# Score masks of the first batch written into PSUM by TensorE, maximum and difference by VectorE from there, the last stores over two queues, and a new order of the instructions

## The chip, the cores and the metric

The kernel runs on one core of one Trainium2 chip. The metric is device time in microseconds (us), lower is better. The engines are TensorE (PE, with its weight loads PEld), VectorE (DVE), ScalarE (ACT), GpSimd (POOL) and SyncE (SP), which issues nearly all DMAs.

## The reference

A sparse attention over 8 heads is followed by a mixture of 4 attention experts. Batch 8, 576 tokens, 8 heads of 64.

```
# stage 1: heads 0-3 see the last 32 tokens, heads 4-7 every 32nd token
scores = 0.125 * q @ k.T
mask_local = (rel >= 0) & (rel < 32)
mask_strided = (rel >= 0) & (pos_k % 32 == pos_q % 32)
scores = where(mask, scores, -1e9); scores -= max(scores)
attn = exp(scores) / (sum(exp(scores)) + 1e-9)
x = concat_heads(attn @ v)                                   # (8, 576, 512)
# stage 2: 4 experts, the best two of a token weighted by a softmax of x @ w_gate
for e in range(4):
    q, k, v = x @ wq[e], x @ wk[e], x @ wv[e]
    a = causal softmax of 0.125 * q @ k.T
    out += gate weight of e * (a @ v @ wo[e])
```

## The kernel before, in words

Stage 1 works on pairs of heads: pairs 0 and 1 of a batch are local, pairs 2 and 3 strided. For a pair q and k are loaded, and in batches 0 and 1 TensorE transposes them (`tp`, L611, L624, L640) and ScalarE or VectorE copies the result from PSUM to `qkt` (`tp_out`, through the helper `copy`, L345). TensorE computes the scores in small blocks, as many as are needed (L673 local, L689 strided), into two PSUM banks `sp`, one for each head. The softmax follows: VectorE adds the mask and writes to SBUF (`p`, L703), takes the maximum (L714), GpSimd subtracts it (L716), ScalarE takes the exponential (L718), VectorE the sums (L720) and their inverse (L723, L725), and GpSimd multiplies (L727). In batch 0 all but the inverse is done head by head. The result is transposed (by VectorE for local pairs, L743, into `pt`; by TensorE for strided ones, L753, and copied), multiplied with v (L783, L802) into `xa`, and split into a high and a low part `xh` and `xl` (L765 ScalarE, L767 VectorE).

Stage 2 projects `xh` and `xl` with the split weights (`wh_k`, `wl_k` and so on, split at L455 and L457). For the first pair of experts of batch 0 the projections are separate matmuls for each head pair (L977), elsewhere in one piece (L966, L895). Then come the experts' scores (L1047, L1059, L1081), masks and maxima (L1016), exponentials (L1021), transposes (L1144), values (L1183) and the output projection (`yp`, L1217), whose result is copied to `ys` and stored (L1227 to L1233).

Nothing of this runs in the order in which it is written. Each step is recorded by `op` (kind, the engines that can do it, what it reads and writes), and `schedule` issues the steps in the order of the table `ORDER`. `SECOND` names the steps that go to their second engine, and `FILL` says before which steps TensorE is given dummy matmuls of 512 columns (L305), whose result nobody reads. Every engine works through its queue in that order, so an instruction that waits holds all behind it. Each queue thus follows the tables; a table's change moves instructions on all engines.

The constants are made first on GpSimd and VectorE: `ident`, `m_loc` (mask of local scores), `m_str` (of strided), and, as steps, `m_cau`, `m_sw` and `m_last` for stage 2.

Of the kernel before, what the change touches and what calls it, by code (L numbers as in the profile page):

```python
# [22 lines left out]
def attention_moe_kernel(  # L23
# [60 lines left out]
    class Ring:  # L84
# [36 lines left out]
    }  # L121
    ORDER = [
# [136 lines left out]
    ]  # L259
    FILL = {  # L260
        7: 1, 17: 7, 80: 4, 132: 3, 134: 3, 139: 1, 216: 2,
    }

    def op(kind, eng, key, fn, r=(), w=(), mode=None, dmas=(), after=()):
# [73 lines left out]
    def dve(n):  # L338
        return 0.07 + 0.00104 * n
# [42 lines left out]
    for hf in range(2):  # L382
        v_ = m_str[64 * hf:64 * hf + 64].rearrange("p (g u) -> p g u", u=NJ)
        keep(v_, [[-NJ, 3], [-1, NJ]], 0, 1)
        keep(v_, [[NJ, 3], [0, NJ]], NJ - 1, -1)
# [909 lines left out]
```

## Time and profile before

The median of three runs is 422.71 us (422.70 to 422.73).

| | |
|---|---|
| the profiled execution's own time | 422.69 us |
| its span (first to last instruction) | 421.0 us |
| TensorE busy | 411.0 us, 98% |
| VectorE busy | 339.8 us, 81% |
| ScalarE busy | 277.5 us, 66% |
| GpSimd busy | 230.3 us, 55% |
| TensorE's granted clock | 0.999 of full |
| chain that ended last: PE, DVE, ACT, DMA | 86%, 5%, 3%, 2% |

The page cuts the span in 40 slices and gives the busy tenths of each engine. TensorE has an 8 in the first three slices (0 to 31.6 us) and a 6 in the last; all between are 9, which stands for 90% and more. The dummy matmuls are counted as busy. The rows below say which stretch, engine or line they are of; a bracket at the end of a row is the idle time before it and what ended it.

### The profile page before, as it was taken

What the parts mean: (1) busy time and instruction counts of PE and PEld (TensorE: products, weight loads), DVE (VectorE), ACT (ScalarE), POOL (GpSimd) and SP (SyncE); (2) the same over time, 40 slices, a digit from 0 to 9 for tenths busy, and PEclk for the clock granted to TensorE, in tenths of its full rate; (3) what the DMA queues carried; (4) which work ended last, traced back from release to release, by engine and by line L of the source; (5) the groups of instructions that cost most, each with busy time, mean ns of one, the idle gap of its engine ahead of it and who ended that gap; (6) DMA issues with size and microseconds to landing.
All of it is one profiled execution on the core that took longest, in us unless ns stands there. A gap on an engine that the chain in (4) does not pass through costs nothing.

```text
span 421.0 us, 18647 instructions
## 1 busy us (share of the span) xinstructions
PE 411.0 (98%) x7523; PEld 358.8 (85%) x7523; DVE 339.8 (81%) x1073; ACT 277.5 (66%) x877; POOL 230.3 (55%) x398
## 2 busy tenths in 40 slices
PE   8889999999999999999999999999999999999996
PEld 5668988987898879998899888998899888997775
DVE  4897898999998899978976699898988896339840
ACT  5677378668776457877767465765666469657862
POOL 5674673776536750699229630589216671185540
PEclk9999999999999999999999999999999999999999
DMA  6667637554656655464356524750443040001033
GB/s 178 194 192 181 121 91 136 100 89 96 112 102 109 146 126 87 94 129 103 72 90 133 134 46 114 129 107 11 114 102 97 20 116 22 2 26 27 27 101 100
DMA packets 156502, 41.86 MB, mean 99 GB/s; under 512 B 146080, under 2 KB 149792, under 8 KB 156416
## 3 DMA queue, kind: packets, MB, share of 16 engines
q1 hardware_dynamic: 156272, 40.54, 43.9%
q8 instruction: 59, 0.97, 1.0%
q14 instruction: 27, 0.22, 0.2%
q10 hardware_dynamic: 144, 0.13, 0.1%
HBM read 31.20 MB, written 9.44 MB: 97 GB/s over the span
## 4 chain that ended last, share of the span: by engine, by line
PE 86%; DVE 5%; ACT 3%; DMA 2%; issue 1%; POOL 1%; SPq 0%; ACTq 0%; POOLq 0%
PE bank L966 22%; PE bank L1217 12%; PE bank L1183 10%; PE bank L895 10%; PE bank L1144 6%; PE bank L1059 5%; PE bank L783 3%; PE bank L802 3%; PE bank L1047 2%; PE bank L689 2%; PE bank L673 2%; PE bank L1081 2%; PE bank L753 2%; PE bank L977 1%; DMA p<-in_q_dram 1%
## 5 line engine op out<-in xcount | busy, mean ns | idle before, releaser
L1021 ACT ACTIVATE p<-p,st 128x384 f32<-128x384 f32 (+3 forms) x128 | 71.5, 561 | 10.8 <-DVE st L1016 10.7
L1117 POOL TENSOR_SCALAR p<-p,st,wt 128x256 f32<-128x256 f32 (+2 forms) x96 | 63.9, 672 | 15.1 <-DVE st L1108 7.4
L1016 DVE CUSTOM_DVE_ANT_0 p<-bank,m_cau 128x384 f32<-128x384 f32 (+2 forms) x96 | 50.0, 548 | 1.2 <-PE bank L1059 0.6
L1183 PE MATMUL bank<-th,vs 128*64 128x192 f32 (+4 forms) x512 | 48.0, 337 | 0.0
L563 DVE STREAM_TRANSPOSE qkt<-nat 128x576 f32<-128x576 f32 x48 | 47.5, 1002 | 0.1
L1183 PEld LDWEIGHTS bank<-th,vs 128*64 128x64 f32 x512 | 33.8, 137 | 13.8 <-issue 7.1
L345 ACT COPY th<-bank 128x256 f32<-128x256 f32 (+2 forms) x108 | 40.4, 434 | 7.6 <-PE bank L1144 7.2
L765 ACT CAST xh<-bank 128x128 fp32r<-128x128 f32 (+4 forms) x112 | 29.4, 320 | 22.3 <-PE bank L783 12.8
L966 PE MATMUL bank<-xh,wh_k 128*128 128x256 f32 (+1 forms) x120 | 36.3, 303 | 0.0
L895 PE MATMUL bank<-wh_v,xh 128*128 128x260 f32 x128 | 36.2, 283 | 0.0
L895 PE MATMUL bank<-wl_v,xh 128*128 128x260 f32 x128 | 36.2, 283 | 0.0
L966 PE MATMUL bank<-xh,wh_q 128*128 128x256 f32 (+1 forms) x120 | 36.1, 301 | 0.1
L767 DVE TENSOR_TENSOR xl<-bank,xh 128x128 fp32r<-128x128 f32 (+4 forms) x112 | 31.8, 322 | 5.3 <-ACT xh L765 5.0
L895 PE MATMUL bank<-wh_v,xl 128*128 128x260 f32 x128 | 35.9, 281 | 0.0
L966 PE MATMUL bank<-xl,wh_k 128*128 128x256 f32 (+1 forms) x120 | 35.5, 296 | 0.0
L966 PE MATMUL bank<-xh,wl_k 128*128 128x256 f32 (+1 forms) x120 | 35.5, 296 | 0.0
L966 PE MATMUL bank<-xl,wh_q 128*128 128x256 f32 (+1 forms) x120 | 35.5, 296 | 0.0
L966 PE MATMUL bank<-xh,wl_q 128*128 128x256 f32 (+1 forms) x120 | 35.5, 296 | 0.0
L1144 PEld LDWEIGHTS bank<-ident,p 64*128 64x128 f32 x800 | 30.2, 139 | 5.7 <-issue 1.3
L716 POOL TENSOR_TENSOR p1l<-p1l,st 128x640 f32<-128x640 f32 (+1 forms) x18 | 20.7, 1151 | 25.7 <-DVE st L714 25.5
L1144 PE MATMUL bank<-ident,p 64*128 64x64 f32 x800 | 33.7, 226 | 0.5 <-DVE p1l L703 0.3
L727 POOL TENSOR_TENSOR p1l<-p1l,st 128x640 f32<-128x640 f32 (+1 forms) x18 | 20.5, 1141 | 18.6 <-DVE st L725 15.2
(190 smaller groups left out, 1220.1 us busy)
## 6 DMA issues: line engine op xcount, KB each, us to landing
nat<-in_q_dram SPq DMA_DIRECT2D x96, 72.0 KB
nat<-in_k_dram SPq DMA_DIRECT2D x96, 72.0 KB
out_dram<-ys SPq DMA_DIRECT2D x23, 256.0 KB
v<-in_v_dram SPq DMA_DIRECT2D x96, 40.0 KB
out_dram<-ys SPq DMA_DIRECT2D x25, 128.0 KB
v<-in_v_dram SPq DMA_DIRECT2D x48, 54.0 KB
v<-in_v_dram SPq DMA_DIRECT2D x32, 48.0 KB
v<-in_v_dram SPq DMA_DIRECT2D x32, 45.0 KB
```

The lines of the kernel that those rows point to most:

```text
L345: (nc.scalar.copy if e == "ACT" else nc.vector.tensor_copy)(dst, src)
L563: op("tq", {"DVE": 0.66 if local else 1.11}, k0 - 13, lambda e, x=x: nc.vector.transpose(turned(qkt.t, x), raw(x) if local else raw(x).rea ...
L765: op("xh", {"ACT": act(n_) + 0.04 * (not local)}, key, lambda e, s_=s_, x_=x_: nc.scalar.copy(x_(xh.t), s_(xa.t)), r=[xa], w=[xh[u]])
L767: op("xl", {"DVE": dve(n_)}, key + 0.5, lambda e, s_=s_, x_=x_: nc.vector.tensor_sub(x_(xl.t), s_(xa.t), x_(f(xh.t))), r=[xa, xh[u]], w=[x ...
L895: nc.tensor.matmul(vp.t[:, :NV], xx.t[:, t0:t0 + 128], ww.t[:, kt, :], start=i == 0, stop=i == 11)
L966: nc.tensor.matmul(pj.t[:, :n_], ww.t[:, kt, ep * 128:(ep + 1) * 128], xx.t[:, c], start=i == 0, stop=i == 11)
L1016: op("max2", {"DVE": 0.08 + 0.00104 * nk}, k_ + 0.5, lambda e, a=a: nc.vector.tensor_tensor_reduce(out=p.t[:, a, :nk], in0=sp[a].t[:, so:s ...
L1021: op("exp2", {"ACT": 0.285 + 0.00084 * nk}, k_ + 1, lambda e, a=a: nc.scalar.activation(p.t[:, a, :nk], p.t[:, a, :nk], AF.Exp, bias=st.t[ ...
L1117: lambda e, p=p, a=a, ci=ci, t=t, nk=nk, s_=s_, ep=ep: nc.gpsimd.tensor_scalar(p.t[:, a, :nk], p.t[:, a, :nk], s_.t[:, 20 + ci + a:21 + ci ...
L1144: nc.tensor.transpose(tp[hf].t[:, 64 * c:64 * c + 64], src, ident[r, r])
L1183: nc.tensor.matmul(acc.t[o, c0:c0 + cn], vw, th[ep, a].t[:, s0:s0 + cn], start=j == 0, stop=j == nj - 1, skip_group_check=True)
L1217: nc.tensor.matmul(yp.t[:, :n_], xx.t[:, c0:c0 + 128], ww.t[:, ep, c], start=i == 0, stop=i == 5)
```

## The change

In batch 0 a step `mk` is added for each head pair: for each of the pair's two banks one bf16 matmul of an identity with the mask (320 columns for a local pair, 324 for a strided one), which starts the accumulation. The score matmuls of batch 0 then accumulate onto it. The addition of the mask on VectorE (L703) goes for batch 0. The maximum is taken from PSUM, and the difference is made by VectorE from PSUM with its result in SBUF; GpSimd no longer subtracts there. Three copies to bf16 (`identb`, `m_strb`, `m_locb`) are made by ScalarE at the start. Stores of the last batch that consist of two transfers become two steps, each of which can go to SP or ScalarE. Batches 1 to 7 keep the mask on VectorE and the difference on GpSimd. `ORDER`, `SECOND` and `FILL` are replaced.

```diff
-        3, 48, 49, 50, 55, 57, 59, 60, 56, 62, 58, 52, 54, 185, 5, 7, 61, 53, 9, 51, 8, 64, 6, 17, 19, 63, 12, 13,
...
     FILL = {
-        7: 1, 17: 7, 80: 4, 132: 3, 134: 3, 139: 1, 216: 2,
+        23: 4, 36: 8, 95: 2, 101: 3, 240: 1,
     }
...
+    m_locb = const.tile([128, 5, 64], BF16, name="m_locb")
+    m_strb = const.tile([128, 54], BF16, name="m_strb")
+    identb = const.tile([128, 128], BF16, name="identb")
+    for x, y in ((identb, ident), (m_strb, m_str), (m_locb, m_loc)):
+        nc.scalar.copy(x, y)
...
+        if b == 0:
+
+            def masked(e):
+                for x in range(2):
+                    nc.tensor.matmul(sp[x].t[:, :ni * nk], identb, m_locb.rearrange("p i c -> p (i c)") if local else
+                                     m_strb.unsqueeze(1).to_broadcast([128, 6, 54]), start=True, stop=False, skip_group_check=True)
+
+            op("mk", {"PE": 0.3}, k0 - 12, masked, w=[*sp], mode=M128)
+
+        kept = {"start": b > 0, "stop": True, "skip_group_check": b == 0}
...
-                            nc.tensor.matmul(o, lhs, rhs, start=True, stop=True)
+                            nc.tensor.matmul(o, lhs, rhs, **kept)
...
-        for h in range(2):
+        for h in range(2 if b else 0):
             op("mask", {"DVE": dve(N // 2)}, k0 - 10, lambda e, h=h: nc.vector.tensor_tensor(
...
-            if step == 0:
+            if b == 0 and step < 2:
+                S_ = sp[h_[0]].t[:, :ni * nk].rearrange("p (i c) -> p i c", c=nk)
+                if step:
+                    nc.vector.tensor_tensor(pv()[:, h_[0]], S_, sv(0)[:, h_[0]].unsqueeze(2).to_broadcast([128, ni, nk]), ALU.subtract)
+                else:
+                    nc.vector.tensor_reduce(sv(0)[:, h_[0]], S_, axis=mybir.AxisListType.X, op=ALU.max)
+            elif step == 0:
...
+            def store(e, parts, c=c):
+                for dst, r in parts:
+                    (nc.scalar if e == "ACT" else nc.sync).dma_start(dst, ys.t[r, c])
+
+            for y, ps in enumerate([[x] for x in parts] if end else [parts]):
+                op("store", {"SP": 0.5, "ACT": 0.5} if end else {"SP": 0.5}, key + h + 1 + 0.1 * y, lambda e, ps=ps, store=store: store(e, ps),
+                   r=[ys[h]], dmas=[(0.4, 0.8 / len(parts))] * len(ps))
```

The tables move instructions in the whole program; three places matter below. The number at a row's start is its place in the engine's queue; the number at a name's end tells tiles apart.

The first is VectorE's queue behind the constants. Before, it copies parts of both local pairs (`qkt_170`, `qkt_172`) and then adds the mask to the first pair's scores:

```order
20 L345 COPY qkt_170<-bank_64 64x64x4 x2
21 L345 COPY qkt_172<-bank_67 64x64x4
22 L345 COPY qkt_172<-bank_68 64x128
23 L345 COPY qkt_172<-bank_69 64x64x4 x2
24 L703 TENSOR_TENSOR p1l_72<-bank_70,m_loc 128x320
25 L714 TENSOR_REDUCE st_184<-p1l_72 128x5
```

In the changed kernel the same queue begins like this (`qkt_176` is the first pair's, `qkt_178` the second's):

```order
20 L344 COPY qkt_176<-bank_64 64x64x4 x2
21 L344 COPY qkt_176<-bank_65 64x64x4
22 L344 COPY qkt_176<-bank_64 64x64x4
23 L344 COPY qkt_176<-bank_65 64x64x4 x2
24 L344 COPY qkt_178<-bank_71 64x64x4
25 L734 TENSOR_REDUCE st_190<-bank_68 128x5
26 L732 TENSOR_TENSOR p1l_72<-bank_68,st_190 128x320
27 L344 COPY qkt_178<-bank_64 64x64x4 x3
```

VectorE now makes six copies of the first pair instead of two, and maximum (L734) and difference (L732) of the first head stand among the copies of the second pair.

The second place is VectorE's transpose of the second local pair (`pt_183` before, `pt_189` after), and what stands ahead of it. Before:

```order
43 L720 TENSOR_REDUCE st_188<-p1s_176 128x6 x2
44 L723 TENSOR_REDUCE st_188<-st_188 128x12
45 L725 RECIPROCAL st_188<-st_188 128x12
46 L767 TENSOR_TENSOR xl_197<-bank_65,xh_192 128x128
47 L767 TENSOR_TENSOR xl_197<-bank_66,xh_192 128x160
48 L743 STREAM_TRANSPOSE pt_183<-p1l_73 128x640
49 L703 TENSOR_TENSOR p1s_179<-bank_71,m_str 128x6x54
50 L714 TENSOR_REDUCE st_190<-p1s_179 128x6
51 L703 TENSOR_TENSOR p1s_179<-bank_68,m_str 128x6x54
```

In the changed kernel (`p1s_185` and `st_196` are the last strided pair's):

```order
46 L734 TENSOR_REDUCE st_196<-bank_71 128x6
47 L745 TENSOR_REDUCE st_192<-st_192 128x10
48 L747 RECIPROCAL st_192<-st_192 128x10
49 L734 TENSOR_REDUCE st_196<-bank_66 128x6
50 L792 TENSOR_TENSOR xl_203<-bank_68,xh_198 128x160
51 L742 TENSOR_REDUCE st_194<-p1s_182 128x6 x2
52 L732 TENSOR_TENSOR p1s_185<-bank_71,st_196 128x6x54
53 L745 TENSOR_REDUCE st_194<-st_194 128x12
54 L747 RECIPROCAL st_194<-st_194 128x12
55 L732 TENSOR_TENSOR p1s_185<-bank_66,st_196 128x6x54
56 L792 TENSOR_TENSOR xl_203<-bank_64,xh_198 128x128
57 L768 STREAM_TRANSPOSE pt_189<-p1l_73 128x640
```

The last strided pair's two maxima and two differences have moved ahead of the transpose.

The third place is the end of ScalarE's queue. Before, ScalarE issues one store:

```order
714 L345 COPY ys_150<-bank_65 128x512
715 L345 COPY ys_151<-bank_68 128x512
716 L345 COPY ys_149<-bank_71 128x256
717 L345 COPY ys_149<-bank_67 128x256
718 L1233 DMA out_dram<-ys_149 128x256
```

In the changed kernel it issues two, and one of the two 256-column copies has gone to VectorE:

```order
706 L344 COPY ys_155<-bank_71 128x512
707 L344 COPY ys_157<-bank_67 128x512
708 L1259 DMA out_dram<-ys_157 64x512
709 L344 COPY ys_156<-bank_70 128x256
710 L1259 DMA out_dram<-ys_156 128x256
```

The store at row 708 stood in SP's queue before.

## Rows read from the trace of the kernel before

**Rows 1.** Busy time by stretch: length, PE, PEld, DVE, ACT, POOL, clock, DMA
```profile
0.00:30.00 30.00, 25.70 (x583) 18.00 (x586) 22.35 (x78) 20.06 (x55) 18.71 (x55) 1.00 0.67 185
8.42:36.91 28.49, 25.47 (x753) 19.59 (x751) 25.52 (x68) 20.21 (x59) 16.11 (x37) 1.00 0.69 195
120.00:400.00 280.00, 279.15 (x4901) 248.17 (x4901) 229.77 (x733) 185.27 (x602) 152.52 (x250) 1.00 0.39 85
400.00:417.00 17.00, 16.95 (x180) 13.06 (x178) 5.72 (x17) 9.22 (x27) 5.10 (x7) 1.00 0.29 91
417.00:421.00 4.00, 0.00 (x0) 0.00 (x0) 0.00 (x0) 0.37 (x1) 0.00 (x0) 0.89 0.54 140
```

**Rows 2.** The chain that ended last: start, length, what
```profile
7.57 1.51 PE bank L305 x7
...
20.82 1.12 POOL p1l L727 x2
...
22.18 1.42 POOL p1s L727 x2
...
24.99 0.69 POOL p1s L716
25.68 1.27 issue
...
26.98 0.74 POOL p1s L716
```

**Rows 3.** VectorE in order of time: start, length, line, output from input
```profile
6.01 0.54 DVE L378 COPY m_loc<-m_loc 128x64 f32<-128x64 f32 x4 [3.24 <-POOL m_loc L362]
...
8.42 2.68 DVE L345 COPY qkt<-bank 64x256 f32<-64x256 f32 x6 [1.81 <-ACT qkt L345]
...
22.25 0.84 DVE L743 STREAM_TRANSPOSE pt<-p1l 128x640 f32<-128x640 f32 x1
...
36.09 0.82 DVE L457 TENSOR_TENSOR wl_q<-th,wh_q 128x256 fp32r<-128x256 f32 x1
```

**Rows 4.** GpSimd in order of time, the constants
```profile
2.31 0.57 POOL L391 MEMSET m_cau<- 128x576 f32 x1
...
4.62 0.29 POOL L362 TENSOR_SCALAR_AFFINE_SELECT m_cau<-m_cau 128x128 f32<-128x128 f32 x1
...
6.92 0.23 POOL L362 TENSOR_SCALAR_AFFINE_SELECT m_loc<-m_loc 32x64 f32<-32x64 f32 x1
```

**Rows 5.** ScalarE in order of time, its first copies
```profile
5.89 4.73 ACT L345 COPY qkt<-bank 64x256 f32<-64x256 f32 x11 [3.82 <-PE bank L611]
```

**Rows 6.** Three lines up to 45 us: shortest/median/longest ns, first and last start
```profile
L703 DVE TENSOR_TENSOR p1l<-bank,m_loc x8: 474/480/492, 11.1 to 37.2; 128x320 f32<-128x320 f32 x8
L714 DVE TENSOR_REDUCE st<-p1s x4: 448/484/491, 17.4 to 26.4; 128x6 f32<-128x324 f32 x4
L716 POOL TENSOR_TENSOR p1s<-p1s,st x4: 730/732/736, 18.1 to 27.0; 128x324 f32<-128x324 f32 x4
```

**Rows 7.** TensorE in order of time
```profile
6.79 0.78 PE L611 MATMUL bank<-ident,p 128*128 128x128 f32 x4
...
22.96 0.40 PE L753 MATMUL bank<-ident,p1s 64*128 64x64 f32 x6 [0.52 <-POOL p1s L727]
...
24.66 1.17 PE L783 MATMUL bank<-pt,v 32*64 32x32 f32 x84
...
42.12 0.77 PE L1047 MATMUL bank<-qk 64*64 64x64 f32 x16
```

**Rows 8.** The last stores: copies on ScalarE, issues on SP and ScalarE
```profile
416.24 0.47 SPq L1227 DMA_DIRECT2D out_dram<-ys  x1
...
416.99 0.37 ACT L345 COPY ys<-bank 128x256 f32<-128x256 f32 x1 [0.29 <-PE bank L1217]
417.40 0.40 ACTq L1233 DMA_DIRECT2D out_dram<-ys  x1
417.44 0.54 SPq L1233 DMA_DIRECT2D out_dram<-ys  x1
```

More of the change, by code (lines that the diff above doesn't have):

```diff
@@ L688, in scores @@
                             lhs, rhs = qg(0, hf ^ x, g, 54), qg(1, hf ^ x, g, 54)
-                        nc.tensor.matmul(o, lhs, rhs, start=True, stop=True)
-        op("sl" if local else "s", {"PE": 0.72 if local else 0.66}, k0 - 11, scores, r=[qkt[0], qkt[1], *([nat[0], nat[1]] if quad and not local else [])], w=[*sp, p[0], p[1]], mode=MS if local else MQ)
+                        nc.tensor.matmul(o, lhs, rhs, **kept)
+        op("sl" if local else "s", {"PE": 0.72 if local else 0.66}, k0 - 11, scores, r=[qkt[0], qkt[1], *([nat[0], nat[1]] if quad and not local else []), *(sp if b == 0 else [])], w=[*sp, p[0], p[1]], mode=MS if local else MQ)
         N = 2 * ni * nk
@@ L738, in stage1 @@
                 r_, w_ = ((ph, sh), (ph + sh, ph), (ph, ph), (ph, sh), (sh, sh), (ph + sh, ph))[step]
+                if b == 0 and step < 2:
+                    eng = {"DVE": dve(n_)}
+                    r_, w_ = [[sp[h_[0]]], [sp[h_[0]], *sh]][step], [sh, ph][step]
                 op(f"softmax{step}", eng, k0 - 9 + step, lambda e, step=step, h_=h_: softmax(step, h_, e), r=r_, w=w_)
@@ L1221, in out_tile @@
             op("yp_out", either(n_), key + h + 0.5, lambda e, yp=yp, c=c: copy(e, ys.t[:, c], yp.t[:, :n_]), r=[yp], w=[ys[h]])
-            def store(e, c=c):
-                t0 = QT[t][0]
-                dma = nc.scalar if e == "ACT" else nc.sync
-                if last:
-                    dma.dma_start(out[b - 1, t0:, :], ys.t[:64, :])
-                    dma.dma_start(out[b, t0:, :], ys.t[64:, :])
-                elif t == 0:
-                    dma.dma_start(out[b, 64:128, :], ys.t[:64, :])
-                    dma.dma_start(out[b, :64, :], ys.t[64:, :])
-                else:
-                    dma.dma_start(out[b, t0:t0 + 128, c], ys.t[:, c])
-            op("store", {"SP": 0.5, "ACT": 0.5} if b == B - 1 else {"SP": 0.5}, key + h + 1, store, r=[ys[h]], dmas=[(0.4, 0.4)] * 2 if last or t == 0 else [(0.4, 0.8)])
+            t0 = QT[t][0]
+            end = b == B - 1
+            if last:
+                parts = [(out[b - 1, t0:, :], slice(0, 64)), (out[b, t0:, :], slice(64, 128))]
+            elif t == 0:
+                parts = [(out[b, 64:128, :], slice(0, 64)), (out[b, :64, :], slice(64, 128))]
+            else:
+                parts = [(out[b, t0:t0 + 128, c], slice(0, 128))]
+            def store(e, parts, c=c):
[4 more added lines that the diff above has]
+                   r=[ys[h]], dmas=[(0.4, 0.8 / len(parts))] * len(ps))
     for hp in START:
```

294 rows, old and new, of tables (ORDER, SECOND) are left out of this document.

## The prediction

> **What bounds the kernel now.** I read the busy time by stretch first. TensorE is busy 279.15 of 280 us from 120 to 400 and 16.95 of 17 up to 417 [rows 1]: there it alone sets the time, and as its matmuls stay the same, a new order can give back little. It is not full in two places. In the first 30 us it is busy 25.70, so 4.30 us are idle, and part of the busy time is filling: 21 dummy matmuls, which in a row of seven take 1.51 us, so 0.216 each [rows 2] and 4.5 in all. Up to the first expert scores at 42.12 [rows 7] some 8.8 us are thus not work. At the end TensorE does nothing for the last 4.0 us [rows 1].
>
> What holds TensorE up at the start is read from the chain of waits. From 20.8 to 27.7 it runs over GpSimd: normalisations (L727), then the last strided pair's two differences (L716), 0.69 and 0.74 us with 1.27 between them [rows 2]. But the stretch from 8.42 to 36.91 shows a second limit beside it: VectorE is busy 25.52 of 28.49 us, GpSimd only 16.11 [rows 1]. The chain names GpSimd; the fuller engine is VectorE. So taking GpSimd off the chain is worth only what VectorE can use.
>
> **The change part by part.** The sum is made against the profiled execution, 422.69 us, of which 1.69 lie around the span of 421.0; the median, 422.71, is the same within 0.02.
>
> *Softmax of batch 0.* VectorE loses 8 mask additions and gains 8 differences. A mask addition, which reads PSUM and a second operand, takes 0.480 us, a maximum from SBUF 0.484 to 0.488 [rows 6]. The difference reads the same operands as the addition, so I cost it at 0.48: VectorE's work is unchanged, 0 us. A maximum from PSUM is not in the trace; the nearest rows are the addition, which reads PSUM (0.48), and the maximum from SBUF (0.484). I take no change; the bounds are those two rows' extremes for one instruction, 0.448 and 0.492 [rows 6], so 8 x 0.044 = 0.35 us either way.
>
> [...]
>
> GpSimd loses 8 differences of 0.73, 5.9 us [rows 6]. On the chain stand only the last two, with the wait between: 25.0 to 27.7, 2.7 us [rows 2]. VectorE is next in line there.
>
> *Masks on TensorE.* Eight matmuls of 320 or 324 columns: at the dummies' 0.216 for 512 columns, 0.135 each, 1.1 us. Three dummies fewer give back 0.65. Both lie in the 8.8 us that are not work; if that cover is gone, the price is 1.1 us.
>
> *Constants.* ScalarE now copies three constants ahead of its first copy of transposes, which began at 5.89 [rows 5]. The last needs the finished local mask, ready at 7.15 before (6.92 + 0.23) [rows 4]; the clearing and cutting of `m_cau` that stood ahead on GpSimd, 0.57 and 0.29, has moved back, so it is ready at about 6.3, and with a 0.4 copy (a copy's length, 4.73/11) ScalarE starts at 6.7, 0.8 late. VectorE covers it: in its new queue six copies of the first pair stand at the head, where before it waited 1.81 us for ScalarE and began at 8.42 [rows 3]. It can now begin at about 5.85, when TensorE's first transposes are there (ScalarE's first copy waited for them until 5.89 [rows 5]); the mask copies of 6.01 to 6.55 [rows 3] come 0.86 earlier and are done by then. The second pair's q, which TensorE took at 6.79 [rows 7], is now loaded behind the first v; this is covered, since the first scores must wait for six copies, until about 8.5.
>
> *VectorE's account up to the last split of the first projections (36.09 + 0.82 = 36.91).* It starts 2.57 us earlier (8.42 - 5.85). It makes four more copies of transposes up to there (17 for 13), 2.68/6 = 0.45 each: 1.8. Were its 2.97 us of idle time unchanged (28.49 - 25.52), it would finish 0.8 earlier. The idle time can shrink: waits on exponentials that queue behind GpSimd are part of it. It can also grow: the first maximum now stands behind a copy and must await the first scores, and the first sum an exponential that queues behind copies on ScalarE. I take 0.7 earlier; ends: 1.75 earlier, if the GpSimd stretch of 2.7 shrinks to two VectorE differences (2.7 - 2 x 0.48), and 1.5 later (third rival). From there to the first expert scores TensorE has about as many projections and transposes left as before and is nearly full, so what VectorE gives goes through: **-0.7 us**.
>
> *The body.* The number of runs of one kind of matmul on TensorE falls from 304 to 297; from 120 to 400 only 0.85 us are idle [rows 1]. A new order can win at most about that and can lose as much by new waits: 0, between -0.7 and +0.7.
>
> *The last stores.* TensorE ends at 417.0; the copy takes 0.37, and ScalarE issues the store at 417.40. SP, held by two stores issued from 416.24, issues its last only at 417.44, for 0.54 us, up to 417.98 [rows 8]. With one of those two on ScalarE, SP is done about 0.5 earlier. ScalarE can take it: it idled 0.29 before its last copy, and another copy of that size, 0.37, goes to VectorE, which leaves 0.66 for an issue of 0.47 [rows 8]. Then ScalarE's store, issued by 417.80, is last, 0.18 earlier, with less queued ahead of it. **-0.3 us**, between 0 and -0.5.
>
> [...] I claim no more than issue time; if the data were the limit the term would be 0 and the time 422.0.
>
> Sum: 422.69 - 0.7 + 0 - 0.3 = **421.7 us**.
>
> **The rivals.** *VectorE gives nothing.* It is 90% busy in the stretch, four more copies are put on it, and each new wait on it is at the front of a full queue. For it: the account leaves 0.8 us, and two new waits of half a microsecond eat it. Against: it held 2.97 us of idle time. Only the stores remain: 422.69 - 0.3 = 422.4.
>
> *GpSimd's stretch goes whole.* The last strided pair's differences are the last link before the K projection can end. If VectorE keeps pace, the start gains the 1.75 above: 422.69 - 1.75 - 0.3 = 420.6. Against: the 90%.
>
> *Slower: the second local pair comes late.* Before, its transpose began at 22.25 and ended at 23.09 [rows 3], and its matmuls ran at 24.66, behind the first strided pair's transposes at 22.96 [rows 7]. In the new queue two maxima and two differences of the last pair stand ahead of it, 4 x 0.48 = 1.9, and five more copies, 5 x 0.45 = 2.25; against 2.57 of earlier start it ends 1.6 later, at 24.7, and at 25.2 with one of the new waits of half a microsecond. Its matmuls then start 0.5 later than at 24.66, and the strided pair's transposes, twice 0.40 [rows 7], come behind instead of ahead, with a dummy of 0.2 placed there: 0.5 + 0.8 + 0.2 = 1.5. From there to 42 TensorE is nearly full, so this comes through: 422.69 + 1.5 - 0.3 = 423.9. It decides if the transpose ends after about 24.5. Against: the last pair is 3 us further by then, so the waits TensorE had for it disappear.
>
> **How the numbers follow.** A measurement of this kernel can tell about 0.2%, 0.85 us, from no change; faster means under 421.86, slower over 423.56. Forecast 0.45, its own range 421.0 to 422.4 (VectorE's half microsecond either way and the body's); three tenths of all chance of it under 421.86, 0.15 above. VectorE gives nothing: 0.20, nearly all in the band. GpSimd's stretch goes whole: 0.15, all faster. Second pair late: 0.20, of which 0.18 slower. So faster 0.45, same 0.35, slower 0.20. The range runs from the second rival's 420.6 less a little of the body to just short of the third's 423.9: 420.3 to 423.8.
>
> **What would show it.** In the changed kernel's profile: VectorE's first copy near 5.9 instead of 8.4; the first scores at about 8.5; VectorE's split of the q weights ending near 36.2; the first expert scores near 41.4 (42.12 before; one block of strided scores now stands ahead of it, 0.8, so it may read 42.2 with the same gain); maxima from PSUM of 0.48; GpSimd without differences of 320 columns; idle time of TensorE from 120 to 400 near 0.85; SP's last store issued before ScalarE's. I am wrong if the transpose of the second local pair ends after 25 and TensorE idles or runs dummies before its matmuls beyond that, if the body's idle time grows by over 0.7, or if the maxima take 0.55 or more.

## The result, and the profile after

The changed kernel takes 428.62 us (427.73 to 430.26, four runs) against 422.72: ratio 1.0144, interval 1.0114 to 1.0175. It is 5.9 us slower, where 421.7 was forecast.

First the stretches of the changed kernel's trace (length, busy time of PE, PEld, DVE, ACT and POOL, clock, DMA):

```profile
0.00:42.00 42.00, 34.64 (x808) 26.99 (x809) 31.90 (x101) 25.49 (x70) 17.99 (x55) 1.00 0.64 172
5.97:38.00 32.03, 26.18 (x759) 20.21 (x759) 26.28 (x72) 21.94 (x63) 10.84 (x26) 1.00 0.66 179
42.00:120.00 78.00, 76.39 (x1630) 67.97 (x1630) 72.70 (x228) 56.11 (x184) 49.56 (x77) 1.00 0.58 111
120.00:400.00 280.00, 276.31 (x4864) 245.87 (x4863) 233.78 (x725) 176.34 (x581) 152.21 (x247) 1.00 0.39 84
400.00:422.90 22.90, 22.90 (x232) 18.09 (x230) 11.97 (x37) 11.90 (x32) 8.25 (x13) 1.00 0.24 78
```

and one stretch of the kernel before:

```profile
40.00:120.00 80.00, 79.40 (x1645) 70.62 (x1644) 73.92 (x230) 56.34 (x180) 48.81 (x76) 1.00 0.57 106
```

TensorE's work that is left at 42.0 us after (76.39 + 276.31 + 22.90 = 375.6) is what was left at 40.0 before (79.40 and [rows 1], 375.5). So the start lost 2.0 us. From there TensorE took 380.9 us after (5.3 idle) and 377.0 before (1.5 idle): the body lost 3.9. The end takes 4.0 in both.

*The start.* VectorE, in order of time (start, length, line, output from input; in brackets the wait before it):

```profile
5.97 3.14 DVE L344 COPY qkt<-bank 64x256 f32<-64x256 f32 x7
9.79 0.49 DVE L734 TENSOR_REDUCE st<-bank 128x5 f32<-128x320 f32 x1 [0.68 <-PE bank L689]
...
11.84 0.87 DVE L344 COPY qkt<-bank 64x256 f32<-64x256 f32 x2 [0.71 <-ACT qkt L344]
...
14.74 0.49 DVE L734 TENSOR_REDUCE st<-bank 128x5 f32<-128x320 f32 x1 [0.72 <-PE bank L689]
...
23.09 0.33 DVE L792 TENSOR_TENSOR xl<-bank,xh 128x160 fp32r<-128x160 f32 x1 [0.92 <-ACT xh L790]
...
25.42 0.83 DVE L768 STREAM_TRANSPOSE pt<-p1l 128x640 f32<-128x640 f32 x1
```

It starts at 5.97 as forecast (8.42 in [rows 3]), but waits for 5.75 us (32.03 - 26.28) up to its last split of the q weights instead of 2.97 [rows 1], and the second local pair's transpose starts at 25.42 (22.25 in [rows 3]). TensorE in the same time:

```profile
8.79 0.96 PE L689 MATMUL bank<-qkt 64*32 64x64 f32 x72 [0.83 <-DVE qkt L344]
...
12.77 1.04 PE L304 MATMUL bank<-ident 128*128 128x512 bf16 x4 [1.61 <-DVE qkt L344]
13.73 0.97 PE L689 MATMUL bank<-qkt 64*32 64x64 f32 x72
...
24.67 1.89 PE L304 MATMUL bank<-ident 128*128 128x512 bf16 x8 [0.55 <-DVE p1s L732]
26.48 1.22 PE L808 MATMUL bank<-pt,v 32*64 32x32 f32 x84
```

The second pair's scores come at 13.73, behind four dummies (L304) that themselves waited 1.61 us; its values come at 26.48, behind eight, where [rows 7] has 24.66.

*The body.* After 44 us TensorE waits eight times for over 0.3 us, 4.8 in all, seven times for VectorE:

```profile
44.44 0.76 PE L705 MATMUL bank<-qkt 64*54 64x54 f32 x42 [0.38 <-ACT qkt L344]
...
47.85 0.36 PE L920 MATMUL bank<-wh_v,xh 128*128 128x260 f32 x1 [0.54 <-DVE st L1041]
...
101.02 0.46 PE L1169 MATMUL bank<-ident,p 64*128 64x64 f32 x8 [0.68 <-DVE th L344]
...
251.16 0.80 PE L1084 MATMUL bank<-qkr 64*128 64x384 f32 x6 [0.52 <-DVE st L1041]
...
296.12 1.63 PE L1208 MATMUL bank<-th,vs 128*64 128x192 f32 x18 [1.34 <-DVE th L344]
...
346.41 0.50 PE L1242 MATMUL bank<-wh_o,oh 128*128 128x512 f32 x1 [0.62 <-DVE xl L792]
...
380.06 0.67 PE L1169 MATMUL bank<-ident,p 64*128 64x64 f32 x13 [0.41 <-DVE qk L344]
...
381.06 0.46 PE L1169 MATMUL bank<-ident,p 64*128 64x64 f32 x7 [0.33 <-DVE ys L344]
```

What VectorE did before the longest of them, and GpSimd beside it:

```profile
293.23 2.22 DVE L945 TENSOR_TENSOR gt<-vs 128x64 f32<-128x64 f32 x1
...
295.59 0.48 DVE L344 COPY th<-bank 128x320 f32<-128x320 f32 x1
```

```profile
292.88 1.28 POOL L749 TENSOR_TENSOR p1s<-p1s,st 128x648 f32<-128x648 f32 x1
294.12 1.26 POOL L749 TENSOR_TENSOR p1l<-p1l,st 128x640 f32<-128x640 f32 x1
```

A comparison of 64 columns (L945, the experts' gates), which takes 0.21 us at its shortest, takes 2.22 and ends at 295.45, just after GpSimd's two multiplications (295.38). The copy that TensorE awaits stands behind it. The waits at 101, 251 and 346 have the same picture: L945 of 1.13 us (GpSimd's L749 ends at 100.45, it at 100.48), the subtraction L1026 of 1.29 instead of 0.49, L945 of 0.97 with L946 of 0.76 behind it. The other three waits for VectorE have smaller ones ahead of them: the one at 47.85 a difference of 16 columns (L462) of 0.40 us, the two at 380 and 381 a copy of two columns that takes 0.16 at its shortest and here 0.73, while GpSimd multiplies (L1142) from 378.76 to 379.53:

```profile
378.81 0.73 DVE L344 COPY wtl<-wt 64x2 f32<-64x2 f32 x1 [0.55 <-POOL wt L965]
```

In the body six of the eight comparisons `gt<-vs` are stretched, by 4.9 us together; before, two of eight, by 1.3.

*The end.* ScalarE's issues of the last stores:

```profile
422.33 0.55 ACTq L1259 DMA_DIRECT2D out_dram<-ys  x1
...
423.49 0.36 ACTq L1259 DMA_DIRECT2D out_dram<-ys  x1
```

SP's last issue ends at 423.42, so ScalarE is last, at 423.85, 0.80 behind TensorE's end (422.77 + 0.28); before, SP was last, 1.0 behind it [rows 8]. The span's end gains only 0.15 of that.

### The profile page after: what moved, and what is told of

Read it like the earlier page. It is cut to its first block, busy times and chain, and to the rows that moved or that the text cites. A ratio compares the mean times of both kernels' runs of the same rounds, so it can differ in the third digit from the quotient of the medians.

```text
span 426.9 us, 18638 instructions
## 1 busy us (share of the span) xinstructions
PE 410.4 (96%) x7528; PEld 358.9 (84%) x7528; DVE 350.4 (82%) x1087; ACT 270.2 (63%) x867; POOL 228.0 (53%) x389
## 4 chain that ended last, share of the span: by engine, by line
PE 89%; DVE 5%; issue 2%; ACT 1%; SPq 1%; DMA 1%; POOL 0%; POOLq 0%; DVEq 0%; ACTq 0%
PE bank L991 23%; PE bank L1242 12%; PE bank L1208 11%; PE bank L920 11%; PE bank L1169 6%; PE bank L1084 4%; PE bank L808 4%; PE bank L689 3%; PE bank L827 3%; PE bank L705 2%; PE bank L1072 2%; PE bank L1106 2%; PE bank L890 1%; PE bank L778 1%; PE bank L304 1%
## 5 line engine op out<-in xcount | busy, mean ns | idle before, releaser
L1046 ACT ACTIVATE p<-p,st 128x128 f32<-128x128 f32 (+3 forms) x128 | 71.7, 563 | 12.7 <-DVE st L1041 12.3
L1142 POOL TENSOR_SCALAR p<-p,st,wt 128x256 f32<-128x256 f32 (+2 forms) x96 | 64.4, 678 | 15.6 <-DVE st L1133 8.3
L344 ACT COPY th<-bank 128x384 f32<-128x384 f32 (+2 forms) x108 | 41.6, 438 | 14.2 <-PE bank L1169 13.4
L792 DVE TENSOR_TENSOR xl<-bank,xh 128x160 fp32r<-128x160 f32 (+4 forms) x112 | 31.9, 321 | 5.0 <-ACT xh L790 4.6
L991 PE MATMUL bank<-xh,wh_q 128*128 128x320 f32 (+1 forms) x120 | 36.0, 300 | 0.0
L749 POOL TENSOR_TENSOR p1l<-p1l,st 128x640 f32<-128x640 f32 (+1 forms) x18 | 20.5, 1144 | 28.9 <-DVE st L747 26.9
L991 PE MATMUL bank<-xh,wh_k 128*128 128x320 f32 (+1 forms) x120 | 35.9, 299 | 0.0
L991 PE MATMUL bank<-xl,wh_k 128*128 128x320 f32 (+1 forms) x120 | 35.5, 296 | 0.0
L991 PE MATMUL bank<-xh,wl_q 128*128 128x320 f32 (+1 forms) x120 | 35.5, 296 | 0.0
L991 PE MATMUL bank<-xl,wh_q 128*128 128x320 f32 (+1 forms) x120 | 35.5, 296 | 0.0
L991 PE MATMUL bank<-xh,wl_k 128*128 128x320 f32 (+1 forms) x120 | 35.5, 296 | 0.0
```

Source lines behind the costliest of these rows:

```text
L344: (nc.scalar.copy if e == "ACT" else nc.vector.tensor_copy)(dst, src)
L792: op("xl", {"DVE": dve(n_)}, key + 0.5, lambda e, s_=s_, x_=x_: nc.vector.tensor_sub(x_(xl.t), s_(xa.t), x_(f(xh.t))), r=[xa, xh[u]], w=[x ...
L991: nc.tensor.matmul(pj.t[:, :n_], ww.t[:, kt, ep * 128:(ep + 1) * 128], xx.t[:, c], start=i == 0, stop=i == 11)
L1046: op("exp2", {"ACT": 0.285 + 0.00084 * nk}, k_ + 1, lambda e, a=a: nc.scalar.activation(p.t[:, a, :nk], p.t[:, a, :nk], AF.Exp, bias=st.t[ ...
L1142: lambda e, p=p, a=a, ci=ci, t=t, nk=nk, s_=s_, ep=ep: nc.gpsimd.tensor_scalar(p.t[:, a, :nk], p.t[:, a, :nk], s_.t[:, 20 + ci + a:21 + ci ...
```

## The experiments

The line numbers of these kernels are up to 5 off those of the changed kernel. Times are medians; the kernel before took 422.4 to 422.9 beside them.

**e1, the changed code in the old order.** Steps new in the code stand where their predecessors did; the difference stands in the place of GpSimd's.

```diff
-    ORDER, SECOND, FILL of the changed kernel
+    ORDER, SECOND, FILL of the kernel before, step by step
```

> The changed code (masks written by TensorE, maximum and difference by VectorE from PSUM, last stores as separate steps), but with the order, the engine choices and the dummy matmuls of the kernel before; each mask step stands right ahead of its scores. Theory A (the new tables cost the time: in the start by dummies and VectorE's queue, in the body by more waits of TensorE on VectorE): 421.5 to 423.2 us, and TensorE idle from 120 to 400 near 0.9 us. Theory B (the softmax of batch 0 on VectorE from PSUM costs the time): 426 us or more.

426.63 us, ratio 1.0095 (1.0075 to 1.0115). Its body is full (279.27 busy from 120 to 400); the loss is in the start, where after waits of 0.82, 0.29, 1.09 and 0.39 us between 22 and 27 the granted clock falls to 0.57:

```profile
28.00:36.00 8.00, 7.82 (x141) 6.63 (x141) 6.24 (x19) 4.32 (x13) 1.99 (x10) 0.57 0.61 182
```

The number is in theory B's range; how much of it is the softmax and how much the clock is left to e10 and e13.

**e2, the old code in the new order.**

```diff
-    ORDER, SECOND, FILL of the kernel before
+    ORDER, SECOND, FILL of the changed kernel, step by step
```

> The code before (masks added by VectorE, difference on GpSimd, no constants in bf16, last stores by SP in pairs), but with the new order, engine choices and dummies; each addition of a mask stands right ahead of its maximum. Theory A: 428 to 430 us, about the changed kernel or slower, since a longer softmax is put into an order made for a shorter one. Theory B: 423 to 424.5 us.

430.71, ratio 1.0207 (1.0181 to 1.0234), just above theory A's range, with the body's idle time (276.74 busy) although nothing of the softmax is changed. The four waits of the changed kernel come again (0.68 us at 103, 0.50 at 253, 1.34 at 298, 0.61 at 347). So the order carries the body's loss. The total is no measure of it, since the clock also fell in the start of this run (0.75 from 10 to 20).

**e3, new start and old body; e4, old start and new body.** The seam is the first scores of the experts.

```diff
 e3: ORDER up to the first experts' scores: changed kernel
-    ORDER, SECOND from there on: changed kernel
+    ORDER, SECOND from there on: kernel before
 e4: the other way round
```

> The changed code; all that the new order issues ahead of the first expert scores (266 steps) stands as in the changed kernel, everything after it in the order and on the engines of before. The trace of the changed kernel puts 2.0 us of its loss ahead of 42 us and 3.9 behind. Theory A with two separate losses: about 424.5 us (422.7 + 2.0 - 0.15), with TensorE's idle time from 120 to 400 back near 0.9 us. Rival (the late start throws the body out of step, so the body's waits come from the start): 427 us or more.

> The changed code; all that the old order issues ahead of the first expert scores (250 steps) stands as before, everything after it in the order and on the engines of the changed kernel. Theory A with two separate losses: about 426.5 us (422.7 + 3.9 - 0.1), TensorE idle from 120 to 400 above 3 us. Rival (the body's waits come from the late start): 422.5 to 423.5 us.

e3 425.09 (ratio 1.0061), 279.28 busy from 120 to 400, clock 1.00: the new start alone costs 2.4. e4 431.03 (1.0203), 276.85 busy. The new body costs 3.5 behind the new start (428.62 - 425.09) and 4.4 behind the old (431.03 - 426.63), 0.77 of it in one wait for a copy of ScalarE right at the seam (46.98 us). e4 lies 4.5 above its theory A, whose sum had left out what the old start loses with the new softmax (e1, 3.9).

**e5, e6, e7: the start, on e3.**

```diff
 e5, TensorE:
+L632, L619 MATMUL bank<-ident,p_169 (second pair) x6
 L692 MATMUL bank<-qkt_176 (first pair's scores)
-L632, L619 MATMUL bank<-ident,p_169 x6
 e6, VectorE:
+L771 STREAM_TRANSPOSE pt_189<-p1l_73 128x640
 L795, two sums, two differences, an inverse
-L771 STREAM_TRANSPOSE pt_189<-p1l_73 128x640
 e7, FILL:
-  second local scores: 4, second local values: 8
```

> The run e3 (new start, old body: 425.09 us) with one move on TensorE: the second local pair's last six transposes (L619, L632), which stand behind the first pair's scores and so wait with them for six copies, stand ahead of them again, as before the change. Theory A, the start loses because the second pair comes through TensorE late: its scores, at 13.72 in e3 and 11.96 before, begin at 12.2 or earlier, and the time falls by 1.0 to 1.7 us, to 423.4 to 424.1. Theory B, VectorE's queue sets the second pair's pace (a maximum and a difference stand among its copies): its scores move by less than 0.5 and the time stays at 424.6 to 425.6.

> e3 (425.09 us) with one move on VectorE: the transpose of the second local pair (L771) stands eleven rows earlier, ahead of the last strided pair's two differences, the sums and the inverse. Theory A, the third rival of the prediction (the second local pair's transpose comes late and TensorE waits for it) is what the start loses: its values, at 25.67 in e3, begin at 24.2 or earlier, and the time falls by 1.0 to 1.7 us, to 423.4 to 424.1. Theory B, the strided pairs come as late and TensorE waits for them instead: the first K projection stays at 30.3 (+-0.3) and the time stays at 424.6 to 425.6.

> e3 (425.09 us) without two of its groups of dummy matmuls: the four ahead of the second local scores and the eight ahead of the second local values. Theory A, these dummies stand in the way of work (they begin only when a bank is free, and the work behind them waits for all of them): the four cost 0.9 and the eight 0.2 to 0.4, the time falls by 0.8 to 1.3 us, to 423.8 to 424.3, with the granted clock at 1.00. Theory B, they hold the clock: without them the granted clock falls under 0.95 between 20 and 45 us, as it did in e1, e2 and e4, and the time rises by 1 us or more, to 426 or above.

e5 426.1 (ratio 1.0069), e6 428.56 (1.012), e7 426.82 (1.0104): none is better than e3's 425.09. In e5 the second scores come at 13.99, no earlier, as its theory B has it; its time is above B's range, and after a wait of 1.43 us the clock fell in this trace (0.78 from 12 to 16, 0.79 from 16 to 20). In e6 the transpose waits 1.24 us for GpSimd's multiplication and holds the split behind it, for which TensorE then waits 1.66: neither theory had that. Here too the clock had fallen, to 0.64 from 12 to 16, but the execution of e6 with the highest mean clock (0.999) took 427.11, so the loss is not the clock's alone. In e7 the scores come at 12.87, but the clock falls twice, after waits of 1.72 and 2.29 us, as theory B has it (of the runs that it names, e1 and e4 fell after 20 us, to 0.52 and 0.50 from 28 to 32; e2 from 8 to 16, to 0.53 and 0.61):

```profile
14.00:18.00 4.00, 4.00 (x26) 3.23 (x26) 2.90 (x9) 2.27 (x6) 1.41 (x2) 0.57 0.85 227
28.00:38.00 10.00, 9.49 (x199) 8.20 (x188) 5.54 (x17) 4.50 (x15) 2.83 (x4) 0.51 0.81 199
```

So these twelve dummies can't all go; the question is where they stand (e12).

**e8, the new order with the old engines in the body.**

```diff
-    SECOND from the experts' scores on: changed kernel
+    SECOND from there on: kernel before
```

> The changed kernel with one part of the tables undone: its order throughout and its engines for the start, but from the first scores of the experts on each step that two engines can do goes to the engine of before (of some 190 such choices of the second engine, 88 are common to both tables). After this point the new body cost 3.5 us (428.62 against 425.09 in e3). Theory A, the engine choices cost it (VectorE has 11 us more work than before, ScalarE 7 less): the time falls to 425.0 to 426.2 and TensorE's idle time from 120 to 400 us, 3.69 in the changed kernel and 0.85 before, to under 1.7. Theory B, the order costs it: the time stays at 427.5 or more and the idle time at 3 us or more; as the order was found with its own engines, it may even be longer.

457.45, ratio 1.0816: theory A fails. The number is in B's open range, but 29 us above the changed kernel it does not show that the order alone cost the 3.5: neither order nor engines can be judged with the other exchanged.

**e9, four moves on VectorE, on the changed kernel.**

```diff
-gate comparison (L945) ahead of a copy th; of th, ol, xl x3; of xl x3
+gate comparison behind them (three places)
-subtraction (L1026) behind two copies th
+subtraction ahead of them (one place)
```

> The changed kernel (428.62 us) with four moves in VectorE's queue in the body and nothing else. In the changed kernel TensorE waits eight times after 44 us, 4.8 us in all, and four of these waits, 0.68 at 101, 0.52 at 251, 1.34 at 296 and 0.62 at 346 us, together 3.16, end with a VectorE instruction that stands right behind one that is stretched: the gates' comparison L945 (1.13, 2.22 and 0.97 us instead of 0.14 to 0.21) and the subtraction L1026 (1.29 instead of 0.49). Each stretched one reads both operands from SBUF and ends when a GpSimd operation that started before it ends. The comparisons are moved behind the awaited copies, the subtraction ahead of two copies. Theory A, these collisions with GpSimd, which the new order makes and the old one mostly missed, cost the body its 3.5 us: the four waits go, TensorE's idle time from 120 to 400 us falls from 3.69 to under 1.6, and the time falls by 2.3 to 3.2 us, to 425.4 to 426.3. Theory B, VectorE as a whole is late (10.6 us more work than before) and the waits return at the next instruction: idle time of 3 us or more and 427.7 us or more.

424.35 (423.80 to 425.87), ratio 1.0042 (1.0026 to 1.0058): 4.3 below the changed kernel, more than the 3.2 of the four waits and than theory A's 2.3 to 3.2. In the traces 3.4 of it lie in the body: from the first scores of the experts to TensorE's end it takes 378.05 us in the changed kernel, 374.68 here, and 374.62 with the old body in e3. The rest of the medians' difference is then the start's, in which nothing was moved and whose time scatters with the clock (last section). The four waits are gone, a new one of 0.52 us stands at 104.0, and the idle time from 120 to 400 is 1.35:

```profile
120.00:400.00 280.00, 278.65 (x4904) 248.43 (x4903) 233.64 (x734) 177.26 (x586) 154.65 (x249) 1.00 0.39 85
```

At the third place VectorE now copies at once, and the comparison, which now comes when GpSimd's multiplications are over, takes 0.22 instead of 2.22:

```profile
293.35 0.49 DVE L349 COPY th<-bank 128x320 f32<-128x320 f32 x1 [0.27 <-PE bank L1174]
...
295.43 0.22 DVE L950 TENSOR_TENSOR gt<-vs 128x64 f32<-128x64 f32 x1
```

**e10, e1 with the clock held.**

```diff
 FILL of e1
+  first strided transposes: 3, second local values: 5, first K projection: 2
```

> e1 (the changed code in the order, engines and dummies of before: 426.63 us) with ten dummy matmuls more: three ahead of the first strided transposes, five ahead of the second local values, two ahead of the first K projection, where TensorE waited in e1 for 0.3 to 1.1 us each between 22 and 28 us, before its granted clock fell to 0.52 to 0.63 from 28 to 36 us. Theory A, the masks on TensorE and the difference on VectorE cost nothing by themselves and e1 lost its time to the clock: with the clock at 1.00 up to 45 us the time is 421.5 to 423.5. Theory B, the new softmax itself costs what e1 lost: 425 us or more although the clock stays at 1.00.

425.82, ratio 1.0075 (1.0062 to 1.0088), with the clock at 1.00: theory A fails, and the number is that of B. It has ten dummies more than e1, though, and the first K projection comes at 29.11 us, against 28.35 in e1. And the last strided pair's differences, in GpSimd's old place, free its two PSUM banks late:

```profile
29.44 0.89 DVE L735 TENSOR_TENSOR p1s<-bank,st 128x324 f32<-128x324 f32 x2
```

**e11, the kernel before with the split stores alone.**

```diff
+ e11: the change's hunk on the stores
+ one 256-column copy to VectorE, one part of the last tile's store to ScalarE
```

> The kernel before (422.7 us) with only the change at its end: stores of two transfers become two steps, the second part of the last tile's store goes to ScalarE, and one of the two last 256-column copies from ScalarE to VectorE, as in the changed kernel. Theory A, the prediction's term of -0.3: 422.3 to 422.5. Theory B, the gap from TensorE's end to the end of the span shrank by only 0.1 in the changed kernel, since the transfer itself sets it and not the issue: 422.5 to 422.8.

422.61 against 422.73, ratio 0.9997 (0.9988 to 1.0005): no difference that can be told; theory B's range.

**e12, four dummies moved, on e3.**

```diff
+L307 MATMUL bank_65<-ident 128x512 x4
 L674 MATMUL bank<-m_locb,identb (the second pair's masks) x2
-L307 MATMUL bank_64<-ident 128x512 x4
 L692 MATMUL bank<-qkt_178 (the second pair's scores)
```

> e3 (new start, old body: 425.09 us) with one group of four dummies moved: from right ahead of the second local scores, where they wait for a bank until 12.8 us and then hold the scores up for 0.96, to ahead of the masks of that pair at 10.4, into the stretch of 10.9 to 12.8 in which TensorE waits. Theory A, the second pair comes late by this: its scores begin at 12.9 instead of 13.72 and the time falls by 0.6 to 1.0, to 424.1 to 424.5, with the clock at 1.00. Theory B, VectorE decides what follows: the scores move but the second local values do not (25.7 +-0.2), and the time stays at 424.8 to 425.4.

424.29, ratio 1.0042 (1.0029 to 1.0055), 0.8 below e3, as theory A has it: the scores begin at 12.88 and the second local values at 24.83 instead of 25.67, with the clock at 1.00. The two ratios' intervals overlap, and the first scores of the experts come only 0.5 earlier in the trace; that e14, with the same move, is again 0.8 below e9 speaks for it.

**e13, the softmax in its old places; e16 and e17, one and two moves more.**

```diff
 e13, VectorE, batch 0, order of before:
-addition of the mask
+maximum from PSUM
-maximum
+difference
 e16:
+L347 COPY pt_188<-bank_65 128x324
 L347 COPY qkt_176<-bank_64
-L347 COPY pt_188<-bank_65 128x324
 e17: also the difference of 26.05 us to behind that copy
```

> The changed code in the order, engines and dummies of before, but other than in e1 and e10 VectorE's queue for batch 0 is kept step by step: the maximum from PSUM stands where the addition of the mask stood, and the difference where the maximum stood. In e1 and e10 the difference stood where GpSimd's had been, for the last strided pair at 29.4 us, and until then it holds the pair's two PSUM banks, written from 21.3 on; before, the addition had freed them by 24.4. Theory A, the new softmax costs nothing and e10's 3.1 us come from this late difference, which keeps two of eight banks and makes TensorE wait: the first K projection, at 29.1 in e10 and 26.6 before, starts at 26.8 or earlier, and the time is 421.5 to 423.2. Theory B, putting the scores' masks on TensorE and keeping the scores in PSUM over two VectorE instructions costs 2 to 3 us wherever the difference stands: 424.7 us or more with the clock at 1.00.

> e13 (423.21 us, the changed code with the softmax in its old places) with one copy moved up by one place in VectorE's queue: the copy of the first strided pair's transposes, for whose PSUM bank TensorE waits 0.66 at 24.7 us in the middle of the second local values, goes ahead of the copy of q's transposes. Theory A, this wait is what e13 has left against the kernel before (it does not exist there), and the clock's fall to half after it in the profiled execution comes with it: the wait falls to 0.3 or less, the clock stays at 1.00 and the time is 422.0 to 422.8, level with the kernel before or just below. Theory B, the new softmax costs its half microsecond elsewhere: 423.0 or more.

> e16 with a second move: the last strided pair's second difference, at 26.05 us in e13, goes up behind the moved copy, so that its bank is free 1 us earlier. Theory A, how long a bank is held is the price of the new softmax: 0.2 to 0.5 below e16. Theory B, the bank is not missed there once the copy is early: level with e16 within 0.3, or later by up to 0.5, since two copies of q's transposes now come behind the difference.

e13 423.21, ratio 1.0015 (1.0005 to 1.0025), at the edge of theory A's range. It has the dummies of e1, without the ten of e10, so the 2.6 below e10 are not the places' alone; against e1, which differs by the places alone, it is 3.4, a part of which is e1's clock. The first K projection, which begins in e1 (28.35) just as its clock falls, comes at 27.19 us. One wait is left inside the second local values, after which the clock was at 0.53 from 27.0 to 29.5 in this execution:

```profile
24.09 0.62 PE L811 MATMUL bank<-pt,v 32*64 32x32 f32 x12
25.37 1.12 PE L811 MATMUL bank<-pt,v 32*64 32x32 f32 x72 [0.66 <-DVE pt L347]
```

In e16 it is gone:

```profile
24.22 1.75 PE L811 MATMUL bank<-pt,v 32*64 32x32 f32 x84
```

e16 422.29 against 422.43, ratio 0.9993 (0.9984 to 1.0002); e17 422.10, ratio 0.9997 (0.9988 to 1.0006). The new softmax costs nothing once the order suits it, and gains nothing that can be told; no version beats the kernel before by more than the measurement.

**e14, the changed kernel with the moves of e9 and e12; e15, old softmax and old start with e9's body and the split stores.**

```diff
 e14: e9
+  FILL of e12
 e15: kernel before, with the change's hunk on the stores
-    ORDER, SECOND from the experts' scores on: kernel before
+    ORDER, SECOND from there on: e9
```

> The changed kernel with the four moves of e9 (424.35 us) and the move of four dummies of e12 (-0.8 us). Theory A, body and start are separate losses and the gains add: 423.3 to 423.8. Theory B, they overlap (work that the start delays less meets the collisions at other places): 424.2 us or more.

> The old softmax and the start of before, with the new body (the order and the engines of the changed kernel from the first scores of the experts on) as e9 has it, with its four moves, and with the split stores. e3 and e9 have the same start; e9's body ends 0.7 us earlier than the old body (424.35 against 425.09). Theory A, the new body is as good as the old one or better once the four collisions are gone: 421.6 to 422.7. Theory B, it hangs on the times at which the new start hands over, and other collisions take the place of the four: 424 us or more.

e14 423.51, ratio 1.0022 (1.0009 to 1.0035): the gains add, and 5.1 of the 5.9 us are back with five moves. e15 423.11, ratio 1.0018 (1.0007 to 1.0029), between its two ranges but 0.4 from A. Without the four collisions the new body is thus level with the old one behind the new start (e9 and e3) and half a microsecond longer behind the old (with the collisions it cost 4.4 there, e4). In the trace of e15 TensorE keeps the times of before to within 0.1 us from 23 to 42 us; then comes the wait at the seam that e4 has too:

```profile
42.83 0.76 PE L693 MATMUL bank<-qkt 64*54 64x54 f32 x42 [0.77 <-ACT qkt L349]
```

## Why the prediction was wrong, by its own steps

*The body, "0, between -0.7 and +0.7".* This step failed first: it is +3.9 in the trace and +3.5 in e3. It took the idle time of 0.85 us from 120 to 400 as what an order can win or lose, and gave the loss the same size as the gain; a full engine bounds only the gain. What stands in its place: VectorE operations on two SBUF operands that began during a GpSimd operation did not end before it in 24 of 25 cases of the changed kernel, the new order makes these meetings at the gates' comparisons (2.22 us at the longest, 0.21 at the shortest), and TensorE awaits what is queued behind them. That this queueing costs the body its time is shown by e9, where four moves on VectorE bring it back; that it is GpSimd that holds these instructions is read from when both end (last section). The trace of before has such meetings, and I had not looked at how an instruction's length varies. One of them is a comparison that took 0.13 us elsewhere, beside GpSimd's L716 from 95.25 to 96.52:

```profile
95.42 1.13 DVE L920 TENSOR_TENSOR gt<-lg 128x16 f32<-128x16 f32 x1 [0.21 <-ACT lg L345]
```

*VectorE's account, "-0.7", with the start.* The first copy at 5.97, the first scores at 8.79 and the maxima of 0.43 to 0.49 us came as forecast; but the account kept 2.97 us of idle time and the queue had 5.75. So VectorE started 2.45 earlier, had 0.76 more work and 2.78 more idle time, and ended its last split 1.1 later (38.00 for 36.91) instead of 0.7 earlier. The third rival named the place: the second local pair's transpose ends at 26.2, beyond its 24.5. Its price of 1.5 was too small, 2.0 to 2.4 measured, and its cause was only partly right. Moving the transpose up alone does not help (e6), since its pair is late from the scores on. Some 0.8 of the loss go with four dummies that stand behind a wait and ahead of awaited scores (e12): "three dummies fewer give back 0.65" counted how many there are, not where they stand. The rest of the start's loss was not traced to single moves; its cause stays open.

*Softmax, masks and constants.* The terms were right in sum: no difference that can be told in e16 and e17, with the maximum from PSUM as long as from SBUF.

```profile
L734 DVE TENSOR_REDUCE st<-bank x8: 432/484/494, 9.8 to 21.7; 128x5 f32<-128x320 f32 x4, 128x6 f32<-128x324 f32 x4
```

(Shortest, median and longest ns.) The medians are level, 0.484 from PSUM here and 0.484 from SBUF for 324 columns in [rows 6], and the longest, 0.494, is under the 0.55 that the prediction set as its limit. But the sum had no term for what e1, e10 and e13 show: where the maxima and differences stand in VectorE's queue moves the first K projection by over a microsecond, and with the clock the whole by 3.4 us (e1 to e13). That the scores' banks, which are now held until the difference has read them, are the reason is argued, not shown: the moves also bring forward all that follows from the differences, and one of them alone, 1.3 us earlier, gained nothing (e17).

*The last stores, "-0.3".* The order of the issues and the 0.2 us of issue time came as forecast; the time gained is 0.15 in the trace, 0.1 in e11, within what cannot be told from no change.

## What to carry to other kernels

Where the busiest engine is idle for 0.85 of 280 us, a new order can win 0.85 there and lose more than that (2.8 here): forecast the two sides apart. Before reordering, list for each line the shortest and the longest duration of one shape on VectorE; here one of 0.21 us (L945, 64 columns) took 2.22 at its longest, and what mattered was who waited behind it (TensorE, 1.34 us). Put dummies where the engine waits anyway and into a bank that is free then, not right ahead of the awaited work: four moved so in e12 came out 0.8 us below e3.

## What the runs showed of the hardware

A VectorE operation on two tensors in SBUF (TENSOR_TENSOR) that started while GpSimd ran one (TENSOR_TENSOR or TENSOR_SCALAR) mostly did not end before it: so in 24 of 25 such cases of the changed kernel and 17 of 22 of the kernel before. The changed kernel's gates' comparisons L945 ended 0.02 to 0.1 us after it, the subtraction of 320 columns at 249.20 ended 0.35 after. The six others began within 0.12 us of the GpSimd operation; beside the one in the changed kernel (376.91) GpSimd's is the longer one, 1.00 us where 0.67 is usual. The comparison at 293.23 ended only after two GpSimd operations in a row (2.22 us for 64 columns). The copy within SBUF of 0.73 at 378.81 looks the same. The profile shows this as a long instruction, not as a wait. Those that read PSUM and SBUF did not show it: of 122 that started in the changed kernel while GpSimd ran one, 62 ended before it. All 28 mask additions of 320 columns (L719) took 0.45 to 0.49 us, among them 14 that began more than 0.12 us into a GpSimd operation; one took 0.48 at 181.55, while GpSimd subtracted from 180.97 to 182.24. Why the two kinds differ is not shown by these runs.

TensorE's granted clock stayed at 1.00 in all stretches shown of the changed kernel, and fell to 0.57 in e1 after waits of 0.29 to 1.09 us and to 0.57 and 0.51 in e7 after waits of 1.72 and 2.29. Such a wait did not always bring it down: e3 and e6 have the same instructions on all engines up to 20 us, with a wait of 1.62 us ahead of 12.8; in e3's profiled execution the clock stayed at 1.00, in e6's it was 0.83 from 10 to 20. The time of e9 scattered with this: its two longest executions (425.83, which is the profiled one, and 425.87) had a mean clock of 0.995, its other four (423.80 to 424.42) 0.998 to 1.000.
